# Another order in three places of a linear-attention and mixture-of-experts kernel: the first loads and scans, the small operations of the routing, and the last three steps with the table of the last tiles

## The chip, the cores and the metric

The kernel runs on one core of one Trainium2 chip, in one launch. The metric is device time in microseconds. The kernel before took 288.81 us (median of three runs, 286.95 to 291.07).

## The reference

Two layers follow each other. The first is a linear attention with a decay: for 4 batches and 8 heads a state of 48x48 is carried over 768 positions. The second is a mixture of 8 experts over the 3072 rows of 384 that come out.

```python
for t in range(S):                                       # attention, q, k, v, alpha: [4, 8, 768, 48]
    state = alpha[:, :, t, :, None] * state + einsum('bhd,bhe->bhde', k[:, :, t], v[:, :, t])
    y[:, :, t] = einsum('bhd,bhde->bhe', q[:, :, t], state)
x = y.transpose(0, 2, 1, 3).reshape(3072, 384)
out = x.copy()                                           # experts
rows = x @ w_skip > 0
e_idx = argmax(x[rows] @ w_gate, axis=1)                 # one expert of 8 for a row
gate = softmax(x[rows] @ w_gate)[e_idx]
h = maximum(x[rows] @ w1[e_idx], 0)                      # 384 -> 1024
out[rows] = x[rows] + gate * (h @ w2[e_idx])             # 1024 -> 384
```

## The kernel before, in words

**Attention.** The 3072 rows are 24 tiles of 128 rows; tile `i` belongs to batch `i % 4` and chunk `i // 4`. A tile's q, k and decays (alpha) lie in one SBUF tile of 112 partitions by 3 x 512 (`qka`, six buffers): columns 0 to 1023 are q and k, columns 1024 to 1535 the decays. For each tile VectorE runs a backward scan of the decays (`decay_rev`, L231; it makes `sfx`) and a forward scan (`decay_fwd`, L246; `pfx`). GpSimd multiplies k by `sfx` (L244) and q by `pfx` (L253), in place. TensorE then makes the scores (L262, into the one bank `ps_s`), VectorE masks them into `st` (`causal`, L269), and TensorE makes the part from the state (`inter`, L299), the new state (`outer`, L309 and L314) and the part from within the tile (`intra`, L323). ScalarE copies the results out of PSUM. `rows` (L345) turns the result back into rows of `x` and, in the same matmuls with the constant `xw`, the 9 logits of each row (8 experts and the skip score); `xw` holds the small input w9 (L110). `copy_x` copies the rows, `logits` (L366) the logits, and `store` (L371) writes the rows out, from SyncE's queue.

**Order.** Nothing reorders the program: each engine runs its instructions in the order in which the Python code writes them (`manual_schedule`), and SyncE's queue holds all loads and stores in that order. The main loop has 21 steps. Step `i` loads tile `i+5`, scans tile `i+3`, makes the scores of tile `i+1`, finishes tile `i`, and makes the rows and logits of tile `i-1`. Three more steps are written out by hand behind the loop.

**Routing.** Tiles are routed in groups: 0 to 5, 6 to 11, 12 to 17, then 18 to 20 (`one`) and 21 to 23 (`two`). For a group, `route_expert` (L378) finds the expert of each row: maximum, comparison, tie break, the choice `m` (L397), and the running counts `cnt`; for the first two groups some of it runs on GpSimd, the counts too (L401), for later ones VectorE does all (L404, L406). `route_rank` (L429) is a matmul over counts and choices that gives each row its place in its expert's list; `route_slot` (L445) makes from it one-hot tiles (`hot`), and `route_vals` (L411) the values to be listed. `table` (L482) multiplies both into a table that holds, for each expert, the numbers and gates of up to 256 rows; `take` adds it up and `ids` (L500 to L502) makes the row numbers `idx`. `route_expert`, `route_vals` and `route_slot` are generators: each `tick()` of the main loop emits one of their small operations, if there is one. In the loop before, the seven ticks of a step stand apart: one between the backward scan and its reciprocal (L239), one behind `decay_rev`, one behind `causal`, one behind `decay_fwd`, one ahead of `logits`, two behind it. The rank matmul of a group (L436) stands in `rows` three steps after its last tile, that is in steps 8, 14 and 20.

**Last tiles.** Expert 0 does not wait for a gather of its rows in the last six tiles: their rows are turned into its input by matmuls with one-hot tiles `hot0` (L465). For that the rows are split into a high and a low part (`late_high`, L542, on ScalarE; `late_low`, L547, on VectorE), and `late_rows` (L524) does both products of one tile. Earlier rows of expert 0 come by an indirect load on GpSimd's queue (L515) and `early_turn` (L530). `first_turn` (L555, L557) copies the sum out as the two parts of expert 0's input.

**Experts.** Each expert has four times `up` (18 matmuls, L665) and two times `down` (24 matmuls, L680) on a high and a low part of inputs and weights. `split_pieces` makes these parts of the weights (L586 on ScalarE, L588 on VectorE), `fetch` loads the weights, `gather(e)` (L515) fetches expert e's rows from the output in two halves, `turn(e)` (L646 to L649) transposes them, and `add` (L688) adds the result, which is scattered back. In the first expert the table of the last six tiles, `take`, `ids` and the gathers of experts 1 and 0 stand behind the first `up`. The load of weights next after the gather of expert 1 waits for that gather (L570). `guard` loads alpha (L622) behind the fourth `up`.

## Time and profile before

| | us |
|---|---|
| median of three runs | 288.81 |
| the profiled execution, whole | 289.72 |
| its span, first to last instruction | 288.0 |
| TensorE busy | 272.3 (95%) |
| VectorE busy | 217.8 (76%) |
| ScalarE busy | 160.1 (56%) |
| GpSimd busy | 124.7 (43%) |

In the profile PE is TensorE's matmuls, PEld its loads of weights, DVE VectorE, ACT ScalarE, POOL GpSimd, SP SyncE; a `q` behind a name is the engine's own queue, where DMAs are issued. A line of a timeline has the start, the duration (of the whole group, where several instructions are merged), engine, line of the kernel, operation, the tile written and those read, the count, and in brackets how long the engine had been idle before and what released it. The granted clock of TensorE stands in the tables by stretches as a share of full speed.

### The profile page before, as it was taken

The numbers are of one execution on the slowest core, as the hardware profiler recorded it, in microseconds if no ns is written. First come the engines' busy times: TensorE is split into PE (matmuls) and PEld (weight loads), VectorE is DVE, ScalarE is ACT, GpSimd is POOL, SyncE is SP. The second block draws the span as 40 slices with busy tenths as digits, with TensorE's granted clock in tenths as the row PEclk, the third lists the DMA queues.
The fourth block names the chain that finished last, engine by engine and source line by source line (L and its number), as shares of the span: only waits on it lengthen the run. The fifth ranks groups of instructions, "written<-read, shape, count | busy, mean of one in ns | idle before, by whom it ended". The sixth has DMA issues, their size and how long they took to land.

```text
span 288.0 us, 7552 instructions
## 1 busy us (share of the span) xinstructions
PE 272.3 (95%) x2905; PEld 254.9 (88%) x2905; DVE 217.8 (76%) x405; ACT 160.1 (56%) x332; POOL 124.7 (43%) x167
## 2 busy tenths in 40 slices
PE   8769999999999999889899999999999999999990
PEld 8658888888888888678799999999999999999990
DVE  7898978898889979969975864938658485766810
ACT  5226564645556455264554549668495785936700
POOL 8656667776578654530661512214131141403011
PEclk9997999999999999999899999999999999999997
DMA  7999998989898846933349975968859597480000
GB/s 212 281 283 212 268 260 216 190 205 199 172 215 194 201 102 204 354 127 100 103 105 377 410 266 167 330 210 265 318 175 339 199 315 291 145 302 31 13 30 21
DMA packets 24971, 60.53 MB, mean 210 GB/s; under 512 B 4142, under 2 KB 10868, under 8 KB 24928
## 3 DMA queue, kind: packets, MB, share of 16 engines
q1 hardware_dynamic: 20576, 50.20, 61.6%
q0 software_dynamic: 2176, 5.05, 5.1%
q10 hardware_dynamic: 2176, 4.72, 5.0%
q8 instruction: 25, 0.41, 0.6%
q14 instruction: 18, 0.15, 0.2%
HBM read 52.94 MB, written 8.65 MB: 214 GB/s over the span
## 4 chain that ended last, share of the span: by engine, by line
PE 50%; DVE 3%; issue 0%; POOL 0%; POOLq 0%; ACT 0%
PE ps_h L665 25%; PE ps_o L680 23%; PE ps_x L646 2%; DVE latel L547 1%; DVE hot L465 1%; DVE hot L470 1%; PE ps_s L524 0%; PE ps_g L524 0%; POOL out_dram L690 0%; DVE o L688 0%; POOLq L837 0%; DVE s L454 0%; DVE s L460 0%; PE ps_f L482 0%; ACT hh L669 0%
## 5 line engine op out<-in xcount | busy, mean ns | idle before, releaser
L690 POOL DMA_INDIRECT out_dram<-o,idx x16 | 17.1, 1068 | 97.7 <-DVE o L688 97.7
L588 DVE TENSOR_TENSOR w1l<-raw,w1h 128x768 fp32r<-128x768 f32 x32 | 29.9, 955 | 21.4 <-ACT w1h L586 21.2
L680 PE MATMUL ps_o<-w2h,hh 128*128 128x384 f32 x128 | 43.4, 339 | 0.0
L680 PE MATMUL ps_o<-w2h,hl 128*128 128x384 f32 x128 | 42.8, 335 | 0.0
L680 PE MATMUL ps_o<-w2l,hh 128*128 128x384 f32 x128 | 42.8, 335 | 0.0
L253 POOL TENSOR_TENSOR qka<-qka,pfx 112x512 f32<-112x512 f32 x24 | 30.6, 1277 | 17.4 <-DVE seed L252 9.9
L665 PE MATMUL ps_h<-xh,w1h 128*128 128x256 f32 x192 | 34.6, 287 | 0.0
L665 PE MATMUL ps_h<-xh,w1l 128*128 128x256 f32 x192 | 34.5, 286 | 0.0
L665 PE MATMUL ps_h<-xl,w1h 128*128 128x256 f32 x192 | 33.9, 287 | 0.0
L244 POOL TENSOR_TENSOR qka<-qka,sfx 112x512 f32<-112x512 f32 x24 | 30.9, 1287 | 4.4 <-DVE sfx L237 3.2
L262 PE MATMUL ps_s<-qka 48*128 48x128 f32 x384 | 28.7, 290 | 3.8 <-POOL qka L253 1.5
L269 DVE COPY_PREDICATED st<-mask,ps_s 128x1024 f32<-128x1024 uint8 x24 | 31.5, 1313 | 0.8 <-PE ps_s L262 0.8
L669 ACT ACTIVATE hh<-ps_h 128x512 fp32r<-128x512 f32 x32 | 19.1, 597 | 21.3 <-PE ps_h L665 21.1
L262 PEld LDWEIGHTS ps_s<-qka 48*128 48x128 f32 x384 | 24.1, 192 | 7.2 <-POOL qka L253 3.2
L237 DVE TENSOR_TENSOR_SCAN sfx<-qka,seed 112x512 f32<-112x512 f32 x24 | 29.2, 1216 | 1.4 <-DMA qka<-in_first_dram 1.4
L588 DVE TENSOR_TENSOR w2l<-raw,w2h 128x768 fp32r<-128x768 f32 x32 | 29.8, 952 | 0.2
L251 DVE TENSOR_TENSOR_SCAN pfx<-qka,seed 112x512 f32<-112x512 f32 x24 | 29.0, 1207 | 0.5
L665 PEld LDWEIGHTS ps_h<-xh,w1h 128*128 128x128 f32 x192 | 28.8, 195 | 0.2
L665 PEld LDWEIGHTS ps_h<-xh,w1l 128*128 128x128 f32 x192 | 28.4, 195 | 0.0
L665 PEld LDWEIGHTS ps_h<-xl,w1h 128*128 128x128 f32 x192 | 28.2, 196 | 0.0
L323 PE MATMUL ps_y<-st,vt 128*48 128x128 f32 (+1 forms) x384 | 27.8, 279 | 0.0
L586 ACT CAST w1h<-raw 128x768 fp32r<-128x768 f32 x32 | 25.7, 831 | 2.5 <-ACT over L631 1.8
(159 smaller groups left out, 538.0 us busy)
## 6 DMA issues: line engine op xcount, KB each, us to landing
raw<-in_w_dram SPq DMA_DIRECT2D x64, 384.0 KB, 4.8
qka<-in_qka_dram SPq DMA_DIRECT2D x36, 288.0 KB, 5.3
vt<-in_v_dram SPq DMA_DIRECT2D x24, 192.0 KB, 5.7
out_dram<-x SPq DMA_DIRECT2D x24, 192.0 KB, 3.6
alpha<-in_nat_dram ACTq DMA_DIRECT2D x8, 576.0 KB, 4.6
qka<-in_first_dram SPq DMA_DIRECT2D x4, 672.0 KB, 10.3
qka<-in_first_dram SPq DMA_DIRECT2D x2, 448.0 KB, 5.2
out_dram<-xr SPq DMA_DIRECT2D x4, 192.0 KB, 4.9
```

The lines of the kernel that those rows point to most:

```text
L237: nc.vector.tensor_tensor_scan(flat(sfx)[:, ::-1], w["qka"][:PD, 2 * SW + 1:QW + 1][:, ::-1], flat(self.seed)[:, ::-1], 0.0, ALU.mult, ALU ...
L244: nc.gpsimd.tensor_tensor(w["kh"][:PD], w["kh"][:PD], sfx[:PD], ALU.mult)
L251: nc.vector.tensor_tensor_scan(flat(pfx), w["qka"][:PD, 2 * SW:QW], flat(self.seed), 0.0, ALU.mult, ALU.max)
L253: nc.gpsimd.tensor_tensor(w["qh"][:PD], w["qh"][:PD], pfx[:PD], ALU.mult)
L262: nc.tensor.matmul(ps[:, h, p * P:(p + 1) * P], lhsT=kh[r, p, :], rhs=qh[r, p, :], start=True, stop=True)
L269: self.nc.vector.copy_predicated(w["st"], self.mask, w["ps"])
L323: nc.tensor.matmul(y, lhsT=w["v"][:, o:o + m], rhs=w["st"][:, h, p * P:(p + 1) * P], start=(i < B and a == 0), stop=(a == NP // 2 - 1))
L586: nc.scalar.copy(out=hi[:, s], in_=raw)
L588: nc.vector.tensor_tensor(lo[:, s], raw, hi[:, s].bitcast(F32), ALU.subtract)
L665: nc.tensor.matmul(ps[:, u, :], lhsT=a[:, k, u * P:(u + 1) * P], rhs=b[:, k, :], start=(n == 0), stop=(n == len(order) - 1))
L669: nc.scalar.activation(out=hh, in_=ps, func=AF.Relu)
L680: nc.tensor.matmul(ps, lhsT=a[:, f, js], rhs=b[:, f, :], start=(n == 0), stop=(n == 3 * FT - 1))
```

## The change

It has three parts.

*First loads and scans.* The loads of the first three tiles are split: decays first (`a`), then q and k (`b`), with the v loads set further back; the constants, and with them the two small loads of w9, stand ahead of the loads of tiles 3 and 4. `decay_fwd(2)` moves from ahead of the main loop into step 0, behind `causal(1)`.

*Routing's small operations.* The seven ticks of a step become five behind `causal` and two behind `logits`.

*Last three steps and the table.* The high parts of tiles 18 and 19 are made earlier and their low parts on GpSimd; the rank matmul of `one` stands behind `rows(21)` instead of `rows(22)`, and its slots and one-hot tiles ahead of `logits(22)`; all high products of `late_rows` come before the low ones, and six of them stand ahead of `rows(23)`; the low parts of tiles 21 and 22 are made later. The bank for odd late tiles becomes wide enough for ranks. In expert 0 the table, `take`, `ids` and the gathers move from behind the first `up` to behind the second.

```diff
-    def load(self, i, part=None):
+    def load(self, i, parts="dv"):
...
+        for part in parts:
+            if part == "v":
+                w["v"] = self.vp.tile([P, DM], F32, name="vt")
+                nc.sync.dma_start(out=w["v"], in_=self.v[i])
+                continue
+            s = {"a": slice(2 * SW, QW), "b": slice(0, 2 * SW), "d": slice(0, QW)}[part]
...
     def decay_rev(self, i):
...
-        self.tick()
         nc.vector.reciprocal(self.seed[:PD, :, 0:1], sfx[:PD, :, 0:1])
...
-            bank = self.ps_v.tile([P, NP * RW], F32, name="ps_v")
+            bank = self.ps_v.tile([P, NP * RW + GT * E], F32, name="ps_v")
...
-    def late_rows(self, i, k):
-        w = self.work[i]
-        for n, part in enumerate(w["parts"]):
-            self.nc.tensor.matmul(self.x0t[k], lhsT=part[:, k * P:(k + 1) * P], rhs=w["hot0"],
+    def late_rows(self, tiles, k, n):
+        for i in tiles:
+            w = self.work[i]
+            self.nc.tensor.matmul(self.x0t[k], lhsT=w["parts"][n][:, k * P:(k + 1) * P], rhs=w["hot0"],
                                   start=(i == LATE and n == 0), stop=(i == NT - 1 and n == 1))
...
-            for i in range(5):
-                for part in range(2) if i < 2 else (None,):
-                    self.load(i, part)
-                if i == 3:
-                    self.nc.sync.dma_start(out=self.a0[:PD], in_=self.a0n)
+            for i, parts in ((0, "ab"), (1, "ab"), (0, "v"), (2, "ab"), (1, "v")):
+                self.load(i, parts)
             self.constants()
+            for i, parts in ((3, "d"), (2, "v")):
+                self.load(i, parts)
+            self.nc.sync.dma_start(out=self.a0[:PD], in_=self.a0n)
+            for i, parts in ((4, "d"), (3, "v"), (4, "v")):
+                self.load(i, parts)
...
             self.decay_rev(2)
-            self.decay_fwd(2)
             self.turn_k(1)
...
                 if i >= 3:
                     self.decay_rev(i + 3)
-                    self.tick()
                 ranked = ends.get(i - 3)
                 self.scores(i + 1)
                 self.causal(i + 1)
-                self.tick()
+                self.tick(5)
+                if i == 0:
+                    self.decay_fwd(2)
                 if i < 3:
                     self.decay_rev(i + 3)
                 self.decay_fwd(i + 3)
-                self.tick()
                 self.inter(i)
...
                         self.small = chain(self.small, self.route_slot(ranked))
-                    self.tick()
                     self.logits(i - 1)
                     self.tick(2)
...
             self.store(i - 2)
+            self.late_high(LATE)
+            self.late_high(LATE + 1)
             self.scores(i + 1)
             self.causal(i + 1)
             self.inter(i)
             self.intra(i)
             self.tick(99)
+            for t in one[:2]:
+                self.late_low(t, self.nc.gpsimd)
             self.scores(i + 2)
...
             self.inter(i + 2)
             self.intra(i + 2)
-            self.late_high(LATE)
-            self.rows(i)
+            self.late_high(one[2])
+            self.rows(i, (one[0], i))
             self.logits(i)
+            slot = self.route_slot((one[0], i))
+            advance(slot, 1)
             self.copy_x(i)
             self.store(i)
-            self.late_low(LATE)
-            self.late_high(LATE + 1)
-            self.rows(i + 1, one)
-            self.late_low(LATE + 1)
-            self.logits(i + 1)
-            slot = self.route_slot(one)
-            advance(slot, 1)
-            self.copy_x(i + 1)
-            self.late_high(LATE + 2)
             advance(slot, 9)
-            self.late_low(LATE + 2)
+            self.late_high(i)
+            self.rows(i + 1)
             ps = self.ps_s.tile([P, 2, NP * P], F32, name="ps_s")
             self.x0t = [ps[:, 0, :CAP], ps[:, 1, :CAP], None]
+            for k in range(2):
+                self.late_rows(one, k, 0)
+            self.logits(i + 1)
+            self.copy_x(i + 1)
+            self.late_low(one[2])
             self.rows(i + 2)
             self.logits(i + 2)
             self.late_high(i + 2)
...
-            self.late_high(i)
             self.late_high(i + 1)
-            self.late_low(i)
             for k in range(2):
-                for t in range(*one):
-                    self.late_rows(t, k)
+                self.late_rows(one, k, 1)
...
             self.late_low(i + 2)
             self.copy_x(i + 2)
-            advance(self.route_slot(two), 9)
+            slot = self.route_slot((i, NT))
+            advance(slot, 9)
+            self.late_low(i)
             self.late_low(i + 1)
             self.x0t[2] = self.ps_g.tile([P, CAP], F32, name="ps_g")
-            for t in range(*one):
-                self.late_rows(t, 2)
+            for n in range(2):
+                self.late_rows(one, 2, n)
             for j in range(NB):
                 self.early_turn(j)
-            for k in range(KT):
-                for t in range(*two):
-                    self.late_rows(t, k)
+            for n in range(2):
+                for k in range(KT):
+                    self.late_rows(two, k, n)
...
                     self.up(e, g)
-                    if (e, g) == (0, 0):
+                    if (e, g) == (0, 1):
                         self.take(self.table(range(LATE, NT), self.ps_f.tile([P, NB * NV * E], F32, name="ps_f")))
                         self.idx, self.g = self.ids(self.const, E), self.gates(self.const)
                         for n in (1, 0):
                             self.gather(n)
                         advance(fetch, 2)
```

More of the change, by code (lines that the diff above doesn't have):

```diff
@@ L213, in warm_up @@
             self.nc.tensor.matmul(ps, lhsT=zero, rhs=zero, start=True, stop=True)
[L215 removed]
+    def load(self, i, parts="dv"):
         nc = self.nc
         t = self.qkab[i % NQ]
[L219 to L229 removed]
+        w = self.work.setdefault(i, {})
+        for part in parts:
[4 more added lines that the diff above has]
+            s = {"a": slice(2 * SW, QW), "b": slice(0, 2 * SW), "d": slice(0, QW)}[part]
+            if i < NQ:
+                nc.sync.dma_start(out=t[:PD, s], in_=self.first[i, :, s])
+            else:
+                for h in range(2):
+                    nc.sync.dma_start(out=t[64 * h:64 * h + D, s], in_=self.qka[i - NQ, h, :, s])
+        w.update(qka=t, qh=t[:, 0:SW].rearrange("p (a t) -> p a t", t=P),
+                 kh=t[:, SW:2 * SW].rearrange("p (a t) -> p a t", t=P))
     def decay_rev(self, i):
@@ L470, in one_hot, with late_slots @@
         return self.nc.vector.tensor_scalar(out=hot, in0=self.slots, scalar1=slot, scalar2=None, op0=ALU.is_equal)
-    def late_slots(self, g):
-        for i in range(*g):
+    def late_slots(self, tiles):
+        for i in tiles:
             yield self.one_hot(i, self.work[i]["slot"])
@@ L518, in fetch_rows @@
             bounds_check=N - 1, oob_is_err=False) for j in range(NB)]
[L520 to L524 removed]
+    def late_rows(self, tiles, k, n):
+        for i in tiles:
+            w = self.work[i]
+            self.nc.tensor.matmul(self.x0t[k], lhsT=w["parts"][n][:, k * P:(k + 1) * P], rhs=w["hot0"],
                                   start=(i == LATE and n == 0), stop=(i == NT - 1 and n == 1))
@@ L924, in static_path @@
             i = NT - 3
-            one, two = (LATE, i), (i, NT)
+            one, two = range(LATE, i), range(i, NT)
+            bank = lambda: self.ps_k.tile([P, NP, PD], F32, name="ps_k").rearrange("p a w -> p (a w)")
             advance(fetch, 2)
             self.store(i - 2)
+            self.late_high(LATE)
+            self.late_high(LATE + 1)
             self.scores(i + 1)
@@ L937, in static_path @@
             advance(split, 1)
-            tab = self.table(range(*groups[-1]), self.ps_k.tile([P, NP, PD], F32, name="ps_k").rearrange("p a w -> p (a w)"))
+            tab = self.table(range(*groups[-1]), bank())
             self.rows(i - 1)
```

25 lines of the change are left out of this document (7 added, 18 removed).

## The prediction, made before the changed kernel was run

> **What bounds the kernel now.** I read the stage table first (busy time of each engine per stretch; columns PE, PEld, DVE, ACT, POOL, PE clock, DMA share, GB/s), then the chain that ended last, then the timelines of the engines where TensorE is not full.
>
> ```profile
> span 288.0 us, 7552 instructions
> ```
>
> ```profile
> 0.00:20.00 20.00, 15.04 (x166) 13.49 (x166) 16.74 (x33) 7.68 (x16) 14.20 (x26) 1.00 0.94 256
> ...
> 40.00:60.00 20.00, 20.00 (x324) 17.43 (x324) 17.00 (x37) 11.19 (x33) 14.70 (x26) 1.00 0.93 212
> ...
> 120.00:140.00 20.00, 18.28 (x202) 16.08 (x198) 17.28 (x68) 10.69 (x23) 6.43 (x15) 1.00 0.42 146
> ```
>
> TensorE is full in the steady attention stage. What an order can win lies in the 4.96 us it is idle in the first 20 us, in 1.72 us between 120 and 140, and in two stretches of half clock:
>
> ```profile
> 18.55:21.96 3.41, 2.01 (x23) 1.66 (x19) 3.23 (x6) 0.97 (x2) 1.97 (x4) 1.00 1.07 279
> 21.96:25.37 3.41, 3.41 (x41) 3.19 (x43) 2.58 (x5) 1.92 (x7) 2.14 (x2) 0.51 1.05 212
> ...
> 141.50:144.91 3.41, 3.41 (x18) 3.41 (x18) 3.31 (x10) 0.05 (x1) 1.55 (x2) 0.50 0.01 4
> 15.14:18.55 3.41, 2.30 (x46) 2.07 (x46) 3.27 (x4) 0.85 (x2) 2.16 (x2) 1.00 1.05 271
> ```
>
> A stretch with 2.01 busy of 3.41 is followed by 3.41 us at half clock, which costs 1.7 us; one with 2.30 busy is not. So a wait of about 1.3 us within one such stretch costs itself and 1.7 more.
>
> **First loads and scans.** TensorE, VectorE, GpSimd and the load queue at the start:
>
> ```profile
> 14.67 0.60 PE L276 MATMUL ps_k<-ident,qka 112*128 112x112 f32 x4 [0.55 <-POOL qka L244]
> 16.39 1.16 PE L262 MATMUL ps_s<-qka 48*128 48x128 f32 x16 [1.11 <-DVE st L269]
> ...
> 20.43 1.11 PE L354 MATMUL ps_g<-xw,xt 112*128 112x105 f32 x8 [1.40 <-DMA xw<-in_w_dram]
> ...
> 21.85 1.98 PE L262 MATMUL ps_s<-qka 48*128 48x128 f32 x16
> ...
> 31.49 1.16 PE L262 MATMUL ps_s<-qka 48*128 48x128 f32 x16
> ```
>
> ```profile
> 12.05 1.22 DVE L237 TENSOR_TENSOR_SCAN sfx<-qka,seed 112x512 f32<-112x512 f32 x1 [1.08 <-DMA qka<-in_first_dram]
> ...
> 23.90 1.31 DVE L269 COPY_PREDICATED st<-mask,ps_s 128x1024 f32<-128x1024 uint8 x1 [0.79 <-PE ps_s L262]
> ...
> 29.43 1.32 DVE L269 COPY_PREDICATED st<-mask,ps_s 128x1024 f32<-128x1024 uint8 x1
> ```
>
> ```profile
> 8.91 1.27 POOL L244 TENSOR_TENSOR qka<-qka,sfx 112x512 f32<-112x512 f32 x1 [0.71 <-DMA qka<-in_first_dram]
> ```
>
> ```profile
> 9.68 2.83 SPq L110 DMA_DIRECT2D xw<-in_w_dram  x2
> ```
>
> The small w9 load stands behind the loads of five tiles, and TensorE waits 1.40 us for it. Moved ahead of tile 3 (two DMAs, past three tile loads, three v loads and a0), it lands well before its use. With v0 behind tile 1, the k multiply of tile 1 loses its 0.71 wait and scores(1) starts about 0.5 earlier. Tile 2's decays land before VectorE needs them, so the 1.08 goes; then comes causal(1) at 12.4, ahead of fwd(2), which runs 13.7 to 14.9, and its q multiply (1.27) ends at 16.2. So scores(2) starts at 16.3 against 16.39: the wait ahead of it only changes its owner, from st to the multiply, and with the earlier TensorE work in front it is about 2.05 long in one piece. Behind it no w9 wait is left, and scores(3) comes at 20.45 instead of 21.85: **-1.4**. Moved loads that come later (v2, v3, v4) are used after their tiles' scores; tile 3 has the w9 packets ahead of it and may land 1 us later, which the slack at scores(3) covers. Bounds: should the half clock not return, VectorE ends the gain: causal(3) to causal(4) took 29.43 - 23.90 = 5.53 with VectorE almost never idle, so causal(4) would start at 22.0 + 5.53 = 27.5 and end at 28.8, and scores(5) follow there instead of at 31.49, -2.65. At the other end -1.25, if tile 3 is late too. I take -1.4 with the half clock still there, since 2.05 is longer than the 1.40 that brought it.
>
> **Routing's small operations.** Seven per step before and after, but five now stand together behind causal, and none ahead of the k multiply. At step 8, where group 0 is ranked:
>
> ```profile
> 50.80 1.27 POOL L253 TENSOR_TENSOR qka<-qka,pfx 112x512 f32<-112x512 f32 x1 [0.71 <-DVE seed L252]
> 52.46 1.58 POOL L401 TENSOR_TENSOR cnt<-cnt,m 128x8 bf16<-128x8 bf16 x6 [0.39 <-DVE m L397]
> ...
> 54.15 1.28 POOL L244 TENSOR_TENSOR qka<-qka,sfx 112x512 f32<-112x512 f32 x1
> ```
>
> ```profile
> 51.65 0.48 DVE L396 TENSOR_TENSOR eq<-eq,m 128x48 f32<-128x48 f32 x1
> ...
> 112.46 1.10 DVE L396 TENSOR_TENSOR eq<-eq,m 128x48 f32<-128x48 f32 x1
> ...
> 125.06 0.18 DVE L396 TENSOR_TENSOR eq<-eq,m 128x24 f32<-128x24 f32 x1
> ```
>
> ```profile
> 55.78 0.19 PE L436 MATMUL ps_g<-cnt,one_b 128*128 128x48 bf16 x1
> ```
>
> The six additions of the counts run before the k multiply of tile 11; now they follow it. The scan of tile 11 (1.22, as at 12.05) starts after eq's end at 52.13 and one operation more, and ends at 53.5; the multiply (1.28) then ends at about 54.95; five additions of 0.26 end at 56.25, and the rank matmul, due at 55.78, waits 0.5. It waits longer, because in step 7 the five operations (two of them on GpSimd, with VectorE waiting for the second) delay the fwd scan by about 0.75 (an estimate: four dependent steps of 0.18, as at 125.06) and so the q multiply from 50.80 to 51.55; eq then meets it at its start, not its end, and takes up to 1.27 instead of 0.48. Everything then comes 0.65 later, a wait of 1.1. Queued behind the rank on TensorE are turn_k and the next scores, so it is lost whole; behind the additions on GpSimd is the q multiply of tile 11, not needed for two steps. Twice (groups 0 and 1): 2.2. Group 2 counts on VectorE: the two count operations now follow causal(21), so TensorE waits at the rank instead of at the next scores. The operations moved off the scan bring causal(21) forward by some 0.5 (an estimate, three of 0.18) and the counts give 0.2 of it back, -0.3; if eq stays blocked for the 1.10 of 112.46 and more, +0.9; +0.3, the middle, taken. Sum **+2.5**, bounds +0.7 and +3.2. In other steps these operations cost nothing: they stand in VectorE's wait for the next logits (17.00 busy of 20 at 40 to 60); without that cover, some 0.1 each.
>
> The Trainium skill (SBUF — State Buffer, the section on the shared ports) says that a VectorE operation with two SBUF inputs and a GpSimd operation that reads SBUF exclude each other, the later one blocked until the first ends; the 0.48 and 1.10 above, for an operation that takes 0.18 alone, agree. By the rule eq would cost its full 1.27 and the sum would be at its middle value, not at its low end.
>
> **Last three steps and the table.**
>
> ```profile
> 130.17 0.19 DVE L366 TENSOR_REDUCE logit<-ps_v 128x9 f32<-128x36 f32 x1
> ...
> 136.64 0.40 DVE L555 CAST xh<-ps_s 128x256 fp32r<-128x256 f32 x1
> ...
> 137.94 0.95 DVE L588 TENSOR_TENSOR w1l<-raw,w1h 128x768 fp32r<-128x768 f32 x1
> ...
> 143.01 0.17 DVE L502 SCALAR_TENSOR_TENSOR idx<-id,none 128x16 uint32<-128x16 f32 x1
> ...
> 143.40 1.82 DVE L588 TENSOR_TENSOR w2l<-raw,w2h 128x768 fp32r<-128x768 f32 x2
> 145.49 0.69 DVE L670 SCALAR_TENSOR_TENSOR hl<-ps_h,hh 128x512 fp32r<-128x512 f32 x1 [0.27 <-ACT hh L669]
> ```
>
> ```profile
> 124.20 1.27 POOL L515 DMA_INDIRECT xr<-out_dram,idx  x1 [3.35 <-DMA raw<-in_w_dram]
> ...
> 143.98 1.33 POOL L515 DMA_INDIRECT xr<-out_dram,idx  x1 [1.86 <-issue]
> 145.61 1.00 POOL L515 DMA_INDIRECT xr<-out_dram,idx  x1 [0.30 <-issue]
> ```
>
> ```profile
> 140.82 0.34 PE L482 MATMUL ps_f<-mv,hot 128*128 128x40 bf16 x7 [0.56 <-DVE hot L470]
> ...
> 149.07 0.33 PE L680 MATMUL ps_o<-w2h,hh 128*128 128x384 f32 x1
> ...
> 153.26 0.81 PE L646 MATMUL ps_x<-ident,xr 128*128 128x128 f32 x6
> ```
>
> ```profile
> 158.23 8.63 PE ps_h L665 x72
> ```
>
> ```profile
> DMA to landing us min/median/max: 2.9/3.8/5.0
> ```
>
> ```profile
> 149.27 0.94 ACTq L622 DMA_DIRECT2D alpha<-in_nat_dram  x2
> ```
>
> The new order gives hot(18..20) to TensorE earlier and puts six high products ahead of rows(23). Those fill its wait, but logits(23) stays near 130.1, and VectorE's work from there to the cast at 136.64 is the same: I take 0 (bounds -0.3 and +0.3). Two subtractions go to GpSimd: by elements about 0.95 each, inside its 3.35 idle before 124.20; without that cover they would hold the first gather up by as much.
>
> Moving the table behind up(0,1) lets up(0,1) start when w1l is there (138.9) instead of behind the table, whose last part starts at 140.82. At 8.63/72 = 0.12 a matmul: up(0,1) to 141.05, table to 141.4, two more ups to 145.7, down(0,0) (153.26 - 149.07 = 4.19) to 149.9. But idx is late next. It now stands on VectorE behind two w2l (1.82) and a hl (0.69): 143.18 + 2.51 = 145.7. GpSimd started the gather 0.8 after idx and the second half 1.63 after the first, so at 148.1; landing took 2.9 to 5.0, and the alpha loads, which follow the fourth up, now fall on top of it. With the median 3.8 the rows are there at 151.9, against 153.26 now: **-1.35**, with TensorE waiting 2.0. Bounds: 2.9 gives -2.25; 5.0 gives -0.15, and 1.7 more if the wait brings half clock, +1.55. The weight loads of w1 issued before the gather no longer wait for it, which only helps.
>
> **The sum.** -1.4 + 2.5 - 1.35 = -0.25. The profiled execution took 289.72 (1.72 around its span), so 289.5; it lies 0.91 above the median of the runs, 288.81, hence **288.6**. A measurement of this kernel tells about 2% from no change: below 283.0 or above 294.6.
>
> **Rivals.** (1) The half clock stays away from both waits: front -2.65, sum -1.5, 287.3. For it: 2.30 busy of 3.41 kept full clock, and a wait can fall across two stretches. Against: both waits are longer than 1.40. The Trainium skill (TensorE: Matmul & The Clock Gate, Part 1) wants an idle window of about 3.4 us for half clock, and so stands with this rival; the row at 18.55 contradicts it, 1.40 idle being enough. (2) The counts come in time (eq not blocked, GpSimd prompt): routing +0.7, sum -2.05, 286.8; with (1) 285.5. For it: 51.65 shows eq blocked only partly. (3) Slower: the gather decides. Its second half lands 5.0 after its issue because of the alpha loads, at 153.1, and the long wait halves the clock: sum -1.4 + 2.5 - 0.15 + 1.7 = +2.65, 291.5. It decides from a landing of 3.5 us on, if half clock follows. Against: they are two DMAs that start before the gather's second half, and 3.8 is the usual landing. (4) The front does nothing, VectorE's chain of scans hiding the moved loads: +1.15, 290.0.
>
> **Chances.** Forecast 0.42; (1) 0.15; (2) 0.18; (3) 0.17; (4) 0.08. The range 285.0 to 291.7 takes in (1), (2) with (1), and (3). Past 2%: faster 0.08 (all low ends at once, -4.2, with the runs' own spread of 1.9 below the median), slower 0.04, within 0.88.
>
> **What would show it.** Right: no wait for xw at the first rows, scores(3) near 20.5; rank matmuls idle about 1 us on GpSimd's counts at steps 8 and 14; no wait at the table; the first turn waiting for gathered rows, at or before 152. Wrong: ranks without a wait; the turn starting straight after down(0,0); scores(3) at 21.8. Full clock in the 20s and at 141 to 155 would make it too slow by 1.7 to 3.4.

## The result and the profile after

The changed kernel took 298.87 us (median of four runs, 295.91 to 299.96), the kernel before 289.56 beside it: a ratio of 1.033, 95% interval 1.027 to 1.039. A second series on another chip gave 1.024 (1.014 to 1.033). It is slower by 2 to 3%; 288.6 had been forecast. The profiled execution took 297.81.

Runs of one kernel differ by the clock that TensorE was granted: over 24 runs of the kernel before in the first series of experiments, spans go from 284.5 at a mean clock of 0.995 to 292.0 at 0.977 (correlation -0.77, slope -275 us per unit of clock, about the span itself). So each series below is also read in two shares: span times clock ("at full clock") and span times one minus clock ("lost to the clock"); both are estimates, since not all of the span is TensorE's. The ratios compare only the runs of each kernel within about 1.5% of its fastest, the shares all of them but one of 1446.67 us.

Line numbers of the changed kernel are 3 or 4 above those of before. The waits of TensorE that matter, in its timeline:

```profile
16.44 2.08 PE L265 MATMUL ps_s<-qka 48*128 48x128 f32 x16 [1.94 <-POOL qka L256]
...
58.08 0.18 PE L439 MATMUL ps_g<-cnt,one_b 128*128 128x48 bf16 x1 [1.33 <-DMA qka<-in_qka_dram]
...
90.48 0.18 PE L439 MATMUL ps_g<-cnt,one_b 128*128 128x48 bf16 x1 [1.31 <-POOL cnt L404]
...
159.74 1.51 PE L650 MATMUL ps_x<-ident,xr 128*128 128x128 f32 x6 [2.07 <-DMA xr<-out_dram,idx]
```

The wait for w9 is gone and so, in this trace, is the wait at the table. In their place stand the 1.94 ahead of the scores of tile 2, one wait for each rank of groups 0 and 1, and 2.07 for the gathered rows. What makes the rank of step 8 late is on GpSimd and VectorE (the load named in the second row is one of several semaphores that the rank's wait joins; the additions of `cnt` end last):

```profile
52.44 1.27 POOL L256 TENSOR_TENSOR qka<-qka,pfx 112x512 f32<-112x512 f32 x1 [1.51 <-DVE seed L255]
...
55.47 1.28 POOL L247 TENSOR_TENSOR qka<-qka,sfx 112x512 f32<-112x512 f32 x1
56.70 1.61 POOL L404 TENSOR_TENSOR cnt<-cnt,m 128x8 bf16<-128x8 bf16 x6
```

```profile
52.46 1.31 DVE L399 TENSOR_TENSOR eq<-eq,m 128x48 f32<-128x48 f32 x1
53.80 0.21 DVE L400 SCALAR_TENSOR_TENSOR m<-logit,eq 128x48 bf16<-128x48 f32 x1
```

`eq` starts with the q multiply and takes all of it, 1.31 where it had taken 0.48, and the count additions start only when the k multiply is done. The table of stretches shows the clock (its third column from the right):

```profile
16.50:19.91 3.41, 3.41 (x39) 3.19 (x41) 3.23 (x5) 0.32 (x1) 1.87 (x2) 0.50 1.04 241
19.91:23.32 3.41, 3.41 (x24) 3.08 (x21) 3.20 (x5) 0.63 (x2) 2.10 (x4) 0.52 1.05 235
...
54.01:57.42 3.41, 2.74 (x44) 2.40 (x41) 3.31 (x7) 0.90 (x2) 1.95 (x5) 1.00 0.95 218
57.42:60.83 3.41, 2.75 (x46) 2.28 (x47) 2.74 (x8) 1.92 (x6) 2.87 (x10) 1.00 0.76 144
...
88.10:91.51 3.41, 2.10 (x21) 1.80 (x22) 2.83 (x8) 1.32 (x3) 2.79 (x11) 1.00 0.99 182
91.51:94.92 3.41, 3.41 (x43) 2.72 (x41) 3.34 (x6) 1.18 (x5) 3.33 (x5) 0.50 0.20 67
94.92:98.33 3.41, 3.41 (x34) 3.08 (x31) 2.11 (x7) 0.90 (x2) 1.27 (x2) 0.50 0.99 190
```

The stretches lie on one grid of 3.41 us. The rank wait of step 8 (56.75 to 58.08) falls across a border at 57.42, both stretches keep 2.74 busy, and the clock stays. That of step 14 (89.17 to 90.48) lies inside one stretch, 2.10 busy, and two stretches at half clock follow, which cost 3.14. The second trace, below, shows that the place on the grid does not decide this alone.

By the starts of the scores, the profiled span grew by 8.1 us so: +0.81 up to tile 9; +3.35 from there to tile 16, the two rank waits with 1.5 each; +3.14 half clock behind the second; +0.45 up to tile 23 (the 0.7 of group 2 in it); -0.22 up to the first up; +0.60 from there to expert 1's first up; nothing behind it.

### The profile page after: what moved, and what is told of

Its sections match the earlier page's. It is cut to its first block, busy times and chain, and to the rows that moved or that the text cites. A ratio compares the mean times of both kernels' runs of the same rounds, so it can differ in the third digit from the quotient of the medians.

```text
span 296.1 us, 7543 instructions
## 1 busy us (share of the span) xinstructions
PE 277.2 (94%) x2905; PEld 259.2 (88%) x2905; DVE 218.9 (74%) x403; ACT 159.8 (54%) x332; POOL 124.3 (42%) x169
## 4 chain that ended last, share of the span: by engine, by line
PE 68%; DMA 14%; DVE 9%; issue 3%; POOL 3%; SPq 1%; ACT 0%; POOLq 0%; DVEq 0%
PE ps_o L684 21%; PE ps_h L669 20%; DMA qka<-in_qka_dram 6%; PE ps_s L265 5%; PE ps_y L326 5%; PE ps_g L357 4%; PE ps_y L302 3%; DMA vt<-in_v_dram 3%; DMA qka<-in_first_dram 2%; DVE sfx L241 2%; PE ps_v L312 2%; DMA xr<-out_dram,idx 2%; PE ps_x L650 2%; PE ps_v L317 2%; PE ps_k L279 2%
## 5 line engine op out<-in xcount | busy, mean ns | idle before, releaser
L684 PE MATMUL ps_o<-w2h,hh 128*128 128x384 f32 x128 | 44.0, 344 | 0.0
L265 PE MATMUL ps_s<-qka 48*128 48x128 f32 x384 | 29.4, 295 | 5.3 <-POOL qka L256 2.7
L669 PE MATMUL ps_h<-xh,w1l 128*128 128x256 f32 x192 | 33.8, 282 | 0.0
L669 PE MATMUL ps_h<-xl,w1h 128*128 128x256 f32 x192 | 33.3, 283 | 0.0
L265 PEld LDWEIGHTS ps_s<-qka 48*128 48x128 f32 x384 | 24.7, 196 | 8.9 <-POOL qka L256 3.3
L326 PE MATMUL ps_y<-st,vt 128*48 128x128 f32 (+1 forms) x384 | 29.2, 288 | 0.0
L669 PEld LDWEIGHTS ps_h<-xh,w1h 128*128 128x128 f32 x192 | 28.2, 191 | 0.5 <-ACT xh L559 0.3
L669 PEld LDWEIGHTS ps_h<-xh,w1l 128*128 128x128 f32 x192 | 27.8, 191 | 0.0
L692 DVE SCALAR_TENSOR_TENSOR o<-ps_o,gates,xr 128x384 f32<-128x384 f32 x16 | 9.8, 615 | 24.2 <-PE ps_o L684 20.7
L669 PEld LDWEIGHTS ps_h<-xl,w1h 128*128 128x128 f32 x192 | 27.5, 191 | 0.0
## 6 DMA issues: line engine op xcount, KB each, us to landing
qka<-in_qka_dram SPq DMA_DIRECT2D x36, 288.0 KB, 5.6
```

The costliest lines, as they stand in the source:

```text
L265: nc.tensor.matmul(ps[:, h, p * P:(p + 1) * P], lhsT=kh[r, p, :], rhs=qh[r, p, :], start=True, stop=True)
L326: nc.tensor.matmul(y, lhsT=w["v"][:, o:o + m], rhs=w["st"][:, h, p * P:(p + 1) * P], start=(i < B and a == 0), stop=(a == NP // 2 - 1))
L669: nc.tensor.matmul(ps[:, u, :], lhsT=a[:, k, u * P:(u + 1) * P], rhs=b[:, k, :], start=(n == 0), stop=(n == len(order) - 1))
L684: nc.tensor.matmul(ps, lhsT=a[:, f, js], rhs=b[:, f, :], start=(n == 0), stop=(n == 3 * FT - 1))
```

## The experiments

All are variants of the kernel before unless the text says otherwise. Differences are those of the means to the kernel before on the same chip; their standard errors are 0.4 to 0.8 us, and 0.4 to 1.6 where there were four or six runs (marked *).

| variant | ratio (95%) | at full clock | lost to the clock |
|---|---|---|---|
| routing only* | 1.026 (1.012-1.040) | +3.6 | +3.4 |
| front only | 1.004 (0.999-1.010) | +0.6 | +1.1 |
| last steps and table only | 0.997 (0.987-1.007) | +1.2 | 0.0 |
| change without routing | 0.999 (0.993-1.005) | +2.2 | -0.7 |
| change, counts first* | 1.024 (1.012-1.036) | +4.4 | -0.2 |
| change, filler at ranks* | 1.020 (1.008-1.033) | +5.9 | +0.8 |
| w9 early | 0.998 (0.994-1.003) | -0.3 | -0.9 |
| last steps, indices early | 1.001 (0.996-1.006) | +1.2 | -1.1 |
| the change again* | 1.024 (1.014-1.033) | +6.5 | +0.9 |
| last steps, indices early, alpha late | 0.993 (0.989-0.997) | -0.8 | -2.1 |
| w9 early and that tail | 0.992 (0.988-0.996) | -1.5 | -1.7 |
| routing, counts first* | 1.010 (1.004-1.017) | +2.9 | -1.4 |
| that, one-hots spread | 1.007 (1.003-1.012) | +1.5 | 0.0 |
| front, w9 last* | none; 293.67 against 288.73 | +1.3 | +2.9 |

**The three parts alone.** Routing only takes the new ticks:

```diff
                 if i >= 3:
                     self.decay_rev(i + 3)
-                    self.tick()
...
                 self.causal(i + 1)
-                self.tick()
+                self.tick(5)
```

> The kernel before with the routing part of the change alone (five operations together behind causal, none ahead of the k multiply). Theory A, the waits at the rank matmuls carry the loss: TensorE waits 1.3 to 1.5 at the ranks of steps 8 and 14 and 0.7 more around step 20, 3.5 to 4 in all, and half clock that follows a rank in some executions adds up to 3.4; 293 to 297. Theory B, the loss is the front's and the gather's: within 1 of the kernel before.

It carries most of the loss. TensorE's timeline and two stretches of it:

```profile
56.75 0.18 PE L435 MATMUL ps_g<-cnt,one_b 128*128 128x48 bf16 x1 [1.32 <-DMA qka<-in_qka_dram]
...
89.18 0.18 PE L435 MATMUL ps_g<-cnt,one_b 128*128 128x48 bf16 x1 [1.33 <-POOL cnt L400]
```

```profile
89.90:93.31 3.41, 3.41 (x36) 2.79 (x38) 3.22 (x7) 1.46 (x6) 3.25 (x6) 0.50 0.21 73
93.31:96.72 3.41, 3.41 (x38) 3.01 (x35) 2.43 (x7) 0.63 (x2) 1.27 (x2) 0.51 0.86 184
```

The same two waits and the same half clock stand there without any other part of the change.

Front only takes the new loads and the later forward scan of tile 2:

```diff
-            for i in range(5):
-                for part in range(2) if i < 2 else (None,):
-                    self.load(i, part)
+            for i, parts in ((0, "ab"), (1, "ab"), (0, "v"), (2, "ab"), (1, "v")):
+                self.load(i, parts)
             self.constants()
+            for i, parts in ((3, "d"), (2, "v")):
+                self.load(i, parts)
```

> The kernel before with the first loads and scans of the change alone. Theory A: scores(2) at 16.4 as before, scores(3) later than before by up to 1.75 with two stretches of half clock, scores(5) at 31.5 to 32.5; time 289 to 291. Theory B: more than 3 slower. As forecast before the run: 1.4 faster.

TensorE's and VectorE's timelines, then a stretch of the loads of this kernel and of the kernel before (last two columns: DMA share, GB/s):

```profile
16.88 1.16 PE L266 MATMUL ps_s<-qka 48*128 48x128 f32 x16 [1.94 <-POOL qka L257]
...
33.17 1.58 PE L266 MATMUL ps_s<-qka 48*128 48x128 f32 x16 [1.73 <-POOL qka L248]
```

```profile
26.87 1.22 DVE L241 TENSOR_TENSOR_SCAN sfx<-qka,seed 112x512 f32<-112x512 f32 x1 [1.31 <-DMA qka<-in_first_dram]
```

```profile
4.00:20.00 16.00, 13.04 (x158) 11.54 (x157) 13.17 (x19) 4.35 (x12) 10.18 (x14) 1.00 1.05 245
```

```profile
4.00:20.00 16.00, 11.88 (x153) 10.31 (x152) 14.21 (x19) 4.51 (x12) 10.92 (x14) 1.00 1.05 282
```

The scores of tile 3 start at 21.11 (21.85 before) and those of tile 4 at 25.84 (27.46 before), at full clock. Then the scan of tile 5 waits 1.31 for its load, that of tile 6 another 0.51, and VectorE's mask of tile 4, which stands behind it, ends at 33.03. The scores of tile 5 wait 1.73 and start at 33.17, later than the 31.49 of before, and half clock follows. At the same DMA share the engines moved 245 GB/s instead of 282.

Last steps and table only:

> The kernel before with the last three steps and the table of the change alone. Theory A: the first up gains 0 to 0.5, the table's wait and the half clock behind it (2.5 to 3.5) go, and the first turn gives it back waiting for gathered rows (2.1) and in half clock (1.5): 288.5 to 290.5. Theory B: more than 2 slower.

GpSimd, ScalarE's queue and TensorE around the first turn:

```profile
148.85 1.07 POOL L515 DMA_INDIRECT xr<-out_dram,idx  x1 [0.30 <-issue]
```

```profile
146.81 0.94 ACTq L623 DMA_DIRECT2D alpha<-in_nat_dram  x2
```

```profile
152.90 0.84 PE L647 MATMUL ps_x<-ident,xr 128*128 128x128 f32 x6 [1.94 <-DMA xr<-out_dram,idx]
```

The table has no wait, and no half clock stands there. The rows land 152.90 - 148.85 = 4.05 after the issue and TensorE waits 1.94. From the first up to expert 1's first up it takes 157.74 - 137.34 = 20.40, against 158.07 - 136.51 = 21.56 before with 1.7 of half clock in it, and 20.04 in a run (counts first alone, below) that has the old tail and no half clock there. At full clock the new tail is slower by 0.4.

The change with the old ticks, that is without the routing part:

> The changed kernel with the routing's small operations put back where they stood. Theory A: the ranks do not wait, and 5 to 7 of the 9.3 lost are back: 290 to 293. Theory B: 296 or more, as changed.

```profile
32.08 1.95 PE L266 MATMUL ps_s<-qka 48*128 48x128 f32 x16 [1.95 <-POOL qka L248]
```

No rank waits. The ratio shows no loss, but at full clock 2.2 us stay (standard error 0.6), so routing is most of the loss and not all of it. The front gives its gain back at tile 5 again.

**Counts first.** The changed kernel, but in steps 8 and 14 one tick stands between the scan and the GpSimd multiplies:

```diff
                                      flat(self.seed)[:, ::-1], 0.0, ALU.mult, ALU.max)
+        self.tick(first)
         nc.vector.reciprocal(self.seed[:PD, :, 0:1], sfx[:PD, :, 0:1])
...
-                self.tick(5)
+                self.tick(5 - first)
```

> The changed kernel with one edit: in steps 8 and 14 one of the five small operations stands between the scan and the GpSimd multiplies again, so that the six count additions precede the k multiply on GpSimd; the other four stay behind causal. Theory (the place of the count additions on GpSimd makes the ranks late): ranks of steps 8 and 14 start without an idle over 0.3 us, no half clock behind step 14, scores(17) near 95 instead of 99.19 in the changed kernel's profile, time 4 to 7 us under the changed kernel, 291.5 to 294. Rival (the five operations in one piece and the blocked eq make the counts late, wherever they stand): each rank still idles about 1.0, half clock stays, 297 or more.

GpSimd's and TensorE's timelines:

```profile
52.72 1.59 POOL L405 TENSOR_TENSOR cnt<-cnt,m 128x8 bf16<-128x8 bf16 x6 [0.38 <-DVE m L401]
...
54.42 1.28 POOL L248 TENSOR_TENSOR qka<-qka,sfx 112x512 f32<-112x512 f32 x1
```

```profile
66.58 1.16 PE L266 MATMUL ps_s<-qka 48*128 48x128 f32 x16 [0.82 <-POOL qka L248]
```

The additions stand ahead of the k multiply, the ranks start without a wait (55.21 and 86.78), the scores of tile 17 at 92.30 instead of 99.19: the order on GpSimd makes the ranks late. The time, 294.68 (291.7 to 297.0), is a little above the theory's range: new waits of 0.8 come at the scores of tiles 12 and 18, and the turn still waits 1.95 for its rows.

**Filler.** The changed kernel with matmuls on zeros ahead of those ranks:

```diff
+        if g1 <= 2 * GT:
+            for _ in range(28):
+                nc.tensor.matmul(pr, lhsT=self.zero[:, :P], rhs=self.zero[:, :n * E], start=True, stop=True)
```

> The changed kernel with 28 small matmuls on zeros ahead of each of the two rank matmuls of groups 0 and 1, written to the rank's own columns; the waits for the counts stay. Theory (a wait of 1.3 us of idle TensorE brings the half clock behind step 14): TensorE is busy ahead of the ranks, the clock stays full from 91 to 98, and the time is about 3 us under the changed kernel, 295 to 296.5, although the counts are as late as before. Rival (the half clock comes from elsewhere, the dense matmuls of the steps for one): the clock falls to half near 91 again and the time is that of the changed kernel, 298 to 299.

```profile
58.37 0.86 PE L440 MATMUL ps_g<-zero 128*128 128x48 bf16 x28
59.87 0.18 PE L442 MATMUL ps_g<-cnt,one_b 128*128 128x48 bf16 x1 [0.63 <-POOL cnt L404]
```

The filler covers 0.86, the wait left is 0.63, and the clock stays full behind both ranks. But it stayed full without filler too in the second trace of the changed kernel, below, so this doesn't tell the theories apart; the loss to the clock, +0.8, is no clear gain on the +0.9 of that series. Inconclusive.

**The change again.** Nothing is edited.

> The changed kernel once more, for more times of it and a second trace. If the profile that the parts were read from is typical, the second one shows the same terms: ranks of steps 8 and 14 idle 1.2 to 1.4 each, half clock behind at least one of them, the first turn waiting about 2 for gathered rows, time 296 to 300. Rival (the loss sits in something that varies from run to run): the terms differ by more than 2 us and other waits take their place.

TensorE's and VectorE's timelines, and the stretches around the ranks' waits:

```profile
56.55 0.18 PE L439 MATMUL ps_g<-cnt,one_b 128*128 128x48 bf16 x1 [1.33 <-POOL cnt L404]
...
88.97 0.18 PE L439 MATMUL ps_g<-cnt,one_b 128*128 128x48 bf16 x1 [1.31 <-POOL cnt L404]
...
145.92 0.34 PE L485 MATMUL ps_f<-mv,hot 128*128 128x40 bf16 x7 [0.87 <-DVE w1l L592]
...
156.85 0.55 PE L650 MATMUL ps_x<-ident,xr 128*128 128x128 f32 x3 [1.27 <-DMA xr<-out_dram,idx]
```

```profile
27.99 1.22 DVE L241 TENSOR_TENSOR_SCAN sfx<-qka,seed 112x512 f32<-112x512 f32 x1 [0.80 <-DMA qka<-in_qka_dram]
```

```profile
53.69:57.10 3.41, 2.08 (x23) 1.67 (x19) 2.96 (x7) 0.88 (x2) 2.84 (x10) 1.00 0.98 204
57.10:60.52 3.42, 3.42 (x70) 3.00 (x68) 3.13 (x7) 1.95 (x7) 3.20 (x7) 1.00 0.46 108
...
87.82:91.23 3.41, 2.26 (x38) 1.86 (x37) 2.83 (x8) 1.92 (x6) 2.72 (x11) 1.00 0.73 160
91.23:94.65 3.42, 3.42 (x54) 3.03 (x52) 3.38 (x9) 1.30 (x3) 2.24 (x3) 1.00 0.67 147
```

The rank waits are the same to 0.02, the first turn waits 0.22 and 1.27 for its two halves, the table waits 0.87, and there is no half clock ahead of 289.21, behind the last matmul. So the waits belong to the kernel, and the half clock behind one of them comes and goes.

The grid does not explain that. In the kernel before the clock falls at 22.01, at 141.47 and, behind the work, at 284.83, that is 35 and 42 steps of 3.413 us apart; so the stretches above are counted back from 289.21 in such steps. On that grid the rank wait of step 8 lies whole in one stretch with 2.08 us busy, less than the 2.10 of the first trace, and no half clock follows. In the kernel before, the half clock at 141.50 even follows a stretch that is 2.46 busy, more than the 2.30 that kept full clock there:

```profile
138.09:141.50 3.41, 2.46 (x24) 1.87 (x23) 3.41 (x9) 2.51 (x4) 3.25 (x6) 1.00 0.39 115
```

The busy time of the one stretch ahead therefore does not tell whether half clock comes; what does is open.

This execution spans 291.6 at a mean clock of 0.996; the kernel before, 288.0 with two half-clock stretches (some 3.4 us), would be about 284.6 without them (an estimate). The difference of 7.0 is there at full clock too. By the same starts, with 1.7 taken off the kernel before for each of the two, it is: +1.0 up to tile 9, from the loads (the scan of tile 6, in the second fence, is 0.80 late, and the scores of tile 5 wait 2.01); +3.4 from there to tile 16, the two rank waits; +1.0 up to tile 23; nothing up to the first up; +1.4 from there to expert 1's first up; +0.3 behind.

**Routing, counts first.** The same edit as above on the routing part alone.

> The kernel before with the routing order of the change, but in steps 8 and 14 one small operation stands between the scan and the GpSimd multiplies again, so that the count additions precede the k multiply; front and last steps as before. Theory (the place of the count additions is the whole cost of the routing part): no rank waits over 0.3, time that of the kernel before, ratio 0.998 to 1.004. Rival (the five operations in one piece behind causal cost something in every step, or at group 2): ratio 1.008 to 1.02, the steps 7 to 20 longer than 4.95 to 5.3 us each.

```profile
66.23 0.49 PE L262 MATMUL ps_s<-qka 48*128 48x128 f32 x4 [0.79 <-POOL qka L244]
```

The rival is right as well: without rank waits 1% stays. Scores 11 to 12 and 17 to 18 take 5.82 and 5.81 instead of 4.95, and 21 to 23 take 8.67 instead of 7.96 (group 2). I blamed the five one-hots that now stand in one piece in steps 9 and 15, and spread them, and group 2's operations, as before:

```diff
+                spread = i in (9, 15, 19, 20)
+                first = 1 if spread or ranked and ranked[1] <= 2 * GT else 0
...
+                    self.tick(spread)
```

> The routing order of the change in steps 7, 8, 13 and 14 with the counts ahead of the k multiply, as in the run with counts first alone; in steps 9 and 15 (one-hots) and 19 and 20 (group 2) the small operations are spread over the step as in the kernel before. Theory (the five one-hots in one piece and the piece at group 2 are the rest of the routing cost): scores(11) to scores(12) and scores(17) to scores(18) take 4.95 again, scores(21) to scores(23) 7.95 to 8.0 instead of 8.67, ratio 0.997 to 1.004. Rival (the pieces in steps 7, 8, 13 and 14 cost as much): ratio still 1.008 or more.

VectorE's and TensorE's timelines:

```profile
50.05 1.30 DVE L396 TENSOR_TENSOR eq<-eq,m 128x48 f32<-128x48 f32 x1
...
63.88 1.31 DVE L269 COPY_PREDICATED st<-mask,ps_s 128x1024 f32<-128x1024 uint8 x1
```

```profile
65.34 1.16 PE L262 MATMUL ps_s<-qka 48*128 48x128 f32 x16 [0.62 <-POOL qka L244]
```

Half right. Scores 21 to 23 are back at 7.92, but 11 to 12 and 17 to 18 still take 5.64, so spreading the one-hots was worth 0.2 each time, and the rest must lie ahead of them, by the order of the edit in the piece in steps 7 and 13. Scores 12 start 0.15 behind the end of VectorE's mask of tile 11 (63.88 + 1.31 = 65.19): VectorE has become the later one there, though the row names a multiply of GpSimd. `eq`, blocked for 1.30 instead of 0.48, holds VectorE 0.8 longer, as much as the 0.69 that is missing; that it is the cause was not tried by itself.

**Front: w9.** The load alone moved, behind tile 2's loads:

```diff
+                if i == 2:
+                    self.constants()
                 if i == 3:
                     self.nc.sync.dma_start(out=self.a0[:PD], in_=self.a0n)
-            self.constants()
```

> The kernel before with the w9 load alone moved: behind the loads of tile 2, ahead of those of tiles 3 and 4. Theory A (the order of the large loads makes tiles 5 and 6 late in the front part): the 1.40 wait for w9 at the first rows is gone, tiles 5 and 6 are in time, scores(5) between 28.4 and 30.1 instead of 31.49, ratio 0.990 to 0.995. Theory B (the small packets of w9 hold the load queue up wherever they stand early): the load of tile 4 is issued about 3 us later, a scan of tile 5 or 6 waits 1 us or more, scores(5) at 31.5 or later, ratio 1.00.

```profile
27.66 1.22 DVE L237 TENSOR_TENSOR_SCAN sfx<-qka,seed 112x512 f32<-112x512 f32 x1 [0.54 <-DMA qka<-in_qka_dram]
```

```profile
30.45 1.16 PE L262 MATMUL ps_s<-qka 48*128 48x128 f32 x16 [1.76 <-POOL qka L244]
```

The w9 wait is gone, and 1.76 stands at tile 5 instead. The reverse, the new front with w9 behind all five tiles:

> The front part of the change with one difference: the w9 load stands behind all five tiles' loads, as in the kernel before; routing and last steps as before. Theory A (the small packets of w9 ahead of the large loads make the tiles late): tile 4's load is issued before 7.5 instead of near 10.1 to 10.8, no scan of tiles 4 to 6 waits over 0.3 for its load, rows(0) waits 1 us or more for w9, scores(5) at 31 to 32. Theory B (the loads are limited by bandwidth, in whatever order they stand): tiles 5 or 6 still wait 0.4 us or more behind their loads although w9 is last. Both give a ratio near 1.00.

```profile
21.47 1.49 PE L358 MATMUL ps_g<-xw,xt 112*128 112x105 f32 x8 [2.65 <-DMA xw<-in_w_dram]
```

No scan of tiles 4 to 6 waits over 0.3 for its load, and the rows wait 2.65 for w9, with half clock behind it: scores 5 at 34.09. It moved 265 GB/s from 4 to 20 us, with w9 early alone it was 273 (282 before, 245 with both), so part of the slower loading is in the order of the large loads. Which packets cost how much was not tried. Both say the same of the stage: the loads have no slack, and a wait taken out at one load comes back at another.

**The tail.** In expert 0 the two w2 splits of the second up follow the gather, so that VectorE makes the indices earlier:

```diff
-                    weights((2, 2, 1, 1)[g], e + g > 0)
+                    if (e, g) != (0, 1):
+                        weights((2, 2, 1, 1)[g], e + g > 0)
...
                         advance(fetch, 2)
+                        weights(2)
```

> The kernel before with the last steps and the table of the change, and one edit more: the two w2 splits of up(0,1) follow the table, its indices and the gather instead of standing ahead of them. Theory (the indices behind the w2 splits on VectorE make the gathered rows late): indices about 2 us earlier, at 144.0 to 144.5 on the scale of the run with the last steps alone (146.25 there), the first turn waits under 0.3 us instead of 1.94, no half clock behind it, up(1,0) near 155.8 instead of 157.74, ratio 0.990 to 0.995. Rival (the landing itself is late, or down(0,0) then waits for its w2 halves): TensorE waits 1 us or more there and the ratio is 0.997 to 1.00.

GpSimd, ScalarE's queue and TensorE:

```profile
149.46 1.35 POOL L515 DMA_INDIRECT xr<-out_dram,idx  x1 [0.30 <-issue]
```

```profile
149.15 1.56 ACTq L623 DMA_DIRECT2D alpha<-in_nat_dram  x2
```

```profile
155.84 0.55 PE L647 MATMUL ps_x<-ident,xr 128*128 128x128 f32 x3 [2.22 <-DMA xr<-out_dram,idx]
```

The rival is right: the second half, issued 0.3 behind the alpha loads, lands 155.84 - 149.46 = 6.4 later. So the alpha loads were moved behind the first turn:

```diff
-                    if (e, g) == (0, FT // 2 - 1):
-                        check = self.guard()
-                        advance(check, 1)
...
+                    if (e, j) == (0, 0):
+                        check = self.guard()
+                        advance(check, 1)
```

> The kernel before with the last steps and the table of the change, the two w2 splits behind the indices (as in the run before), and one edit more: the first two alpha loads are issued behind the first turn instead of behind the fourth up. Theory (the alpha loads, issued between the indices and the gather's second half, take the DMA engines and make its rows land 5 to 6.5 us after the issue): the second half lands in 3 to 4 us, both halves of the first turn start within 0.3 us of down(0,0)'s end, up(1,0) some 2.4 us earlier relative to up(0,0) than in the run with the indices early alone (there 160.41 - 139.68 = 20.7, so 18.3 here), ratio 0.990 to 0.996. Rival (landing of 5 us or more comes from the weight loads that run beside it): the wait of 2 us stays, ratio 0.998 to 1.004.

```profile
147.73 1.35 POOL L515 DMA_INDIRECT xr<-out_dram,idx  x1 [0.30 <-issue]
```

```profile
151.14 0.82 PE L647 MATMUL ps_x<-ident,xr 128*128 128x128 f32 x6
```

Both halves are there at 151.14, at most 3.4 after the issue, without a wait; ratio 0.993. The table still waits 0.81 in this trace. With w9 early as well:

> The kernel of the run with late alpha loads, and the w9 load behind tile 2's loads as in the run with that alone; routing as in the kernel before. Theory (the two gains are in separate stages and add): ratio 0.985 to 0.993, no wait for w9, none at the table, under 0.5 at the first turn. Rival (a gain in the front is given back at the scores of tiles 5 and 6, whose loads are late, and half clock follows one of the waits): ratio 0.995 to 1.00.

Its first up to expert 1's first up takes 157.14 - 138.84 = 18.30, and w9 and the turn have no wait. The ratio, 0.992, is hardly below that of the tail alone, and the scores of tile 5 wait 1.38 in it: the front adds nothing that can be told. Both versions are 0.7 to 0.8% faster than the kernel before, with intervals that leave out no change, and 3 to 4% faster than the changed kernel (medians 286.95 and 286.87 against 289.48 and 298.23). Most of the 2.9 us between the means of the first and of the kernel before is time lost to the clock (2.1), so what the late alpha loads are worth is less sure than the wait that they remove.

## Why the prediction was wrong

*Routing (+2.5).* The mechanism came as forecast: counts behind the k multiply, `eq` blocked for the whole q multiply, TensorE idle at both ranks. The sizes were low: a wait of 1.33 and 1.31, 1.5 with the restart, where 1.1 stood; group 2 +0.7 (8.67 against 7.96), where 0.3 stood. Alone the part costs 3.6 at full clock (standard error 0.6), and 4.4 stand between tiles 9 and 23 of the second trace, both above the upper bound of 3.2. A step was also left out of the sum: the text had read from the trace that a wait of about 1.3 inside one stretch costs 1.7 more, priced it for the front and the gather, and never set it against the two waits that it forecast for the ranks. In the first trace, and in that of the part alone, one of them brought 3.1; in the second trace neither did. Twice 1.7 would have put the upper bound at 6.6; the part alone measured +7.0 in all (3.6 and 3.4).

*Front (-1.4).* The wait of 2.05 in one piece came as 1.94, and at full clock the scores of tile 3 start at 20.62 (second trace; forecast 20.45). Two steps failed. The later loads were held to be covered: w9 was followed to tile 3 only, not through the queue to tiles 5 and 6, whose loads then came late. In the second trace the stage is 1.2 ahead at tile 3 and 1.0 behind from tile 5 on. And the half clock was put at its old price, but lasted 6.8 us instead of 3.4 in the first trace, which set tile 3 back to 23.60. Alone the part costs +0.6 and +1.1. The fourth rival, no gain from the front, was nearest, though by the loads and not, as it said, by VectorE's scans.

*Last steps and table (-1.35).* The last three steps were worth 0 (-0.22 measured), there was no wait at the table in the first trace (0.87 in the second), and the wait for gathered rows was 2.07 where 2.0 stood: right in the main. From the first up to the first turn the forecast gave 151.9 - 136.51 = 15.4, the trace gives 159.74 - 144.04 = 15.7. What failed is the half clock behind that wait, which stood only in the upper bound and in the third rival: it came at 159.7 in the first trace and not in the run of the part alone. The forecast gain was less than the 1.7 of half clock that this part removes and then risks again: at full clock the tail costs 0.5 alone (20.40 against 21.56 - 1.7) and 1.4 in the second trace.

*The sum.* -0.25 forecast, +8.1 in the profiled execution. **The steps that failed are these: the moved loads were taken as covered, the two rank waits were put too low, and the half clock behind the ranks was left out.** The last is the largest single term of the first trace, 3.14, but it does not decide: the second trace has no half clock and is 7.0 behind all the same. Taken at full clock, the forecast comes to -0.25 + 1.7 = +1.45, since it let one of the two half-clock stretches of before go. Of the 5.6 that are missing in the second trace, the front is 2.4, the routing 1.9 and the tail 1.0; 0.3 stand behind expert 1's first up. The routing's share is shown by experiment (with the counts first the rank waits go); the shares of front and tail are read from traces.

By the runs: the three parts alone add to +5.4 at full clock, the whole change has +6.5, with standard errors near 1; the share lost to the clock is +4.5 and +0.9, too scattered to say more of. The third rival, slower because the gather decides, had the direction but the wrong place; routing is most of the loss, 4.4 of the 7.0. The first rival, that the clock stays full, happened in the second trace, the fastest of its series with 293.30, and even that is slower than the kernel before (289.48 on that chip). The prediction's price of half clock rested on two stretches of one trace, 2.01 and 2.30 busy; the 2.46 at its own second place, and the 2.08 of the second trace, contradict it.

The Trainium skill (TensorE: Matmul & The Clock Gate, Part 1) says that the activity window of about 3.4 us runs freely, not from the kernel's start; the grid of the first trace agrees. It also asks for an idle window before half clock; here a wait of 1.31 us in a stretch 2.10 busy of 3.41 was followed by it, so the measurement decides.

## What to carry to other kernels

Every wait that a prediction forecasts on TensorE has to be followed by the question what the clock does behind it, with the same price at each place and a chance: here the same wait brought half clock in one execution and none in another. An operation moved in the program is moved on every queue at once: what matters is which long instruction it now stands behind, here six small additions behind one k multiply. In a stage whose loads have no slack, and at a gather that shares the DMA engines with other loads, a removed wait returns at the next load unless something is taken out of its way.

## What the hardware showed beyond that

Half clock lasted two stretches (6.8 us) behind waits in the attention stage and one (3.4) behind those of the experts in the first trace; in the kernel before it lasted one at 21.96. Why two is open. In the run of the front with w9 last a wait of 2.65 was followed by two again (22.06 to 28.88), and in that of the last steps with the indices early there were three in a row (18.07 to 28.31).

The time from the issue of a gather's second half to its rows went with how shortly before it the alpha loads had been issued on another queue: at most 3.4 us with none ahead, 4.05 and 4.2 with them 2.0 ahead (last steps alone; the first trace of the change, 155.53 to 159.74), 5.15 with them 1.0 ahead (its second trace), 6.4 with them 0.3 ahead. The run with late alpha loads tried it; the rest is a comparison between kernels.
